# Attention and a SiLU feed-forward on one core: other byte offsets between the operands that TensorE streams and the weights that it loads

## The chip, the cores and the metric

The kernel runs on one core of a Trainium2 chip. The metric is device time in microseconds (us) of one execution, as the median of several. Lower is better.

## The reference

Eight batches of eight heads, 576 tokens, head size 64, go through attention with a mask by blocks of 64; the 4608 tokens of 512 features that come out go through a feed-forward with SiLU, without a bias. All is float32.

```python
B, H, S, D = q.shape                      # 8, 8, 576, 64
scores = (1.0 / np.sqrt(D)) * np.matmul(q, k.transpose(0, 1, 3, 2))
mask = (pos[:, None] // 64) >= (pos[None, :] // 64)
scores = np.where(mask, scores, -1000000000.0)
attn = np.exp(scores - np.max(scores, axis=-1, keepdims=True))
attn = attn / (np.sum(attn, axis=-1, keepdims=True) + 1e-09)
x = np.matmul(attn, v).transpose(0, 2, 1, 3).reshape(B * S, H * D)
h = x @ w_in                              # 4608x512 by 512x2048
out = (h / (1.0 + np.exp(-h))) @ w_out    # 4608x2048 by 2048x512
```

## The kernel before, in words

All instructions stand in one written order, the table `ORDER`; each word of it calls one method, and each engine works through its own instructions in that order. Float32 operands of the two feed-forward products are split into a high part in the rounded type float32r and a low part (the rest), and a product is made of three matmuls: high by high, high by low, low by high.

**Features and W_in.** `wi` (W_in, high and low, 64 KiB each in a partition) stays in SBUF throughout. Behind it stands a gap of `HALF_LINE` = 16 floats (64 bytes), and then `xbuf`, 64 KiB, that holds the features x. All pieces of W_in that TensorE loads start at a multiple of 256 bytes from the start of `wi`, and all pieces of x at a multiple of 256 bytes from the start of `xbuf`, so that x lies at 64 bytes from W_in modulo 256. The last 448 tokens of each batch are a group ("b", b): `x_batch(b)` gives its place, batch after batch in the two halves of `xbuf` in turn, as 4 chunks of features by high and low by 448 tokens (1792 bytes, 7 times 256). `x_hi` (ACT, L853) and `x_lo` (GpSimd, L856) write it once for two heads. The first 128 tokens of all batches make four more blocks of 256 tokens, which `x_batch` doesn't place.

**First product.** `ffn1` (the word `ffn` in `ORDER`, L1096) does a step: for a batch and one of 16 pieces of 128 columns of W_in, 12 matmuls of 128x128 weights from `wi` and 448 streamed columns from x, in two halves. A batch has 16 steps, 192 matmuls; eight batches have 1536 of the 1968 matmuls of L1096. `keep` takes a step's result out of PSUM, `save` sends it to DRAM.

**Attention.** For each of 64 heads, `scores` (L739) does ten matmuls: five pieces of the queries' columns (448, 320, 192, 448 and 64), each first with the high part `qh` and then with the low part `ql`, and with the keys, which lie in the same tile as `qh`, as the weights that are loaded. In that tile queries and keys are a multiple of 256 bytes apart; `ql` stands 64 bytes further (L723).

**Second product.** Here the parts of W_out stream and the features g are loaded. W_out is stored as eight double steps (`Turned`, d = 0 to 7) of two times seven blocks of 256 columns: d = 0 and 1 in tiles `ta`, d = 2 to 6 in tiles `tb`, d = 7 in the first half of `xbuf`. An `Item` is a quarter of a block of 256 tokens; it has two double steps, d = 2q and 2q + 1 for its quarter q, and puts its features into one of five places in turn: four in `wi`, which is no longer needed, and a fifth in the second half of `xbuf` (`slots`, L1190). `prod` (L1185) does one of the item's seven products: five of them are four matmuls in the order of 512, 512, 256 and 256 streamed columns, two are six of 256. There are 72 items; in the last four all products have six of 256.

```python
    def slots():
        if not spare:
            spare.extend([of_wi(d, d + 1) for d in (0, 4, 2, 6)] + [of_x(8, HALF_LINE)])
        return spare
```

Before, all of W_out lies at 64 bytes from `wi` modulo 256, and at 192 from the fifth place.

Of the kernel before, what the change touches and what calls it, by code (L numbers as in the profile page):

```python
# [10 lines left out]
F32R = mybir.dt.float32r  # L11
# [9 lines left out]
P = 128  # L21
NQ = S - 2 * D
# [9 lines left out]
CT = DM // P  # L32
# [41 lines left out]
PRODUCTS = [(1, 0), (2, 1), (6, 5), (5, 3), (7, 4), (3, 6), (4, 2)]  # L74
LAST = [(1, 0), (6, 5), (7, 4), (5, 3), (2, 1), (3, 6), (4, 2)]
HALF_LINE = 16
NARROW = (3, 4)
WIDE_WALKS = {"a": (0, 1, 2, 3), "b": (0, 2, 1, 3), "c": (1, 0, 3, 2)}
NARROW_WALKS = {"a": (0, 1, 2, 3, 4, 5), "b": (0, 3, 1, 4, 2, 5)}
WALKS = ("bb bb bb bb",)  # L80
FACTOR = {5: 0, 7: 1, 6: 2, 4: 3, 1: 4, 2: 5, 3: 6}

# [388 lines left out]
def attn_ffn(ctx: ExitStack, tc: tile.TileContext, qk, v, qk0, v0, qk1, v1, w_in, w_out, out):  # L471
# [14 lines left out]
    def bank(i):  # L486
        return pS.tile([P, 512], F32, tag=f"S{i}", name=f"S{i}")
# [5 lines left out]
    wi = [wboth[:, t] for t in range(2)]  # L493
    fp.tile([P, HALF_LINE // 2], F32, tag="gap", name="gap")
    cp.tile([P, HALF_LINE], F32, name="gap")
    xbuf = cp.tile([P, NX, 2, TB], F32R, name="x")
# [11 lines left out]

    def x_batch(b):
        half = xbuf[:, 8 * (b % 2) : 8 * (b % 2) + 8].rearrange("p n i t -> p (n i t)")  # L510
        return half[:, : CT * 2 * NQ].rearrange("p (c i t) -> p c i t", c=CT, i=2)

    def x_of(g, c, i):
        if g[0] == "b":
            return x_batch(g[1])[:, c, i]
        x = xbuf[:, 4 * g[0] + c, i, :]
        return x if len(g) == 1 else two(x, 4 * 2 * TB)
# [89 lines left out]
    def groups(seven):  # L607

        return [seven[:, 0:2], seven[:, 2:3], seven[:, 3:5], seven[:, 5:7]]
# [5 lines left out]
    def of_wi(d, e):  # L615

        a, b = slice(256 * d, 256 * d + 256), slice(256 * e, 256 * e + 256)
        return [[w[:, 0:2, a], w[:, 2:3, a], w[:, 0:2, b], w[:, 2:4, b]] for w in wi]

    def of_x(n, o):  # L620

        t = xflat[:, 2 * TB * n + o : 2 * TB * (n + 7) + o].rearrange("p (k i t) -> p k i t", i=2, t=TB)
        return [groups(t[:, :, i]) for i in range(2)]

    class Turned:
# [10 lines left out]
        def place(u):  # L636
            if u.d < NTA:
                t = pools["ta"].tile([P, 2, 7, 256], F32R, tag=f"ta{u.d}", name="ta")
                u.g = [groups(t[:, i]) for i in range(2)]
            elif u.d < 7:  # L640
                t = sp.tile([P, 2, 7, 256], F32R, tag=f"tb{u.d}", name="tb")
                u.g = [groups(t[:, i]) for i in range(2)]
            else:
                u.g = of_x(0, 0)
# [46 lines left out]
    class Unit:  # L691
# [30 lines left out]
        def split_q(u):  # L722
            u.ql = sp.tile([P, 512 + HALF_LINE], F32R, tag="ql", name="ql")[:, HALF_LINE : HALF_LINE + NQ]  # L723
            nc.gpsimd.tensor_tensor(out=u.ql, in0=u.raw[:, :NQ], in1=u.qh[:, :NQ], op=ALU.subtract)  # L724
            u.kk = u.qh[:, NQ:]
# [36 lines left out]
        def spread(u):  # L762
            for a in range(1, 4):
                copies[COPIES[1]](out=u.m[32 * a : 32 * a + 32], in_=u.m[:32])
# [85 lines left out]
        def x_hi(u):  # L850
            own(("b", u.b), u.h // 2)
            u.x = x_batch(u.b)[:, u.h // 2]
            nc.scalar.copy(u.x[:, 0], u.xu)  # L853
# [255 lines left out]
    class Item:  # L1109
# [53 lines left out]
        def prod(u, i):  # L1163
# [4 lines left out]
            o = z.o[pr]  # L1168
            second = z.wide and pr == NARROW[1]
            runs = []  # L1170
# [10 lines left out]
            kind = WALKS[u.blk % len(WALKS)].split()[u.q]  # L1181
            order = WIDE_WALKS[kind[0]] if len(runs) == 4 else NARROW_WALKS[kind[1]]
            for n, k in enumerate(order):
# [6 lines left out]
# [5 lines that stand above are left out]
    class Out:  # L1195
# [7 lines left out]
        def spread(u, pr):  # L1203
            return u.wide and pr not in NARROW

        def place(u, pr):

            if pr == NARROW[1]:
                return u.both[:, HD:] if u.wide else bank(3)
            if pr in (2, NARROW[0]):  # L1210
                t = pH.tile([P, 512], F32, tag="h", name="c2")
                if pr == NARROW[0]:
                    u.both = t
# [70 lines left out]
    a, b = First(0), First(1)  # L1284
# [24 lines left out]
    for token in ORDER.split():  # L1309
        name, _, method = token.partition(".")  # L1310
        if name.startswith("warm:"):
            warm(int(name[5:]))
        elif method:
            method, _, k = method.partition(":")
# [47 lines left out]
```

## Time and profile before

| what | value |
|---|---|
| median of 3 runs | 973.15 us (972.49 to 973.54) |
| profiled execution | 971.61 us, span in the trace 969.9 us |
| PE (matmuls) | 960.1 us busy, 99% of the span |
| PEld (weight loads) | 842.4 us, 87% |
| DVE, ACT, POOL | 810.0 us (84%), 688.4 us (71%), 644.1 us (66%) |
| granted clock of TensorE | 1.0 of full speed (2.4 GHz) |

The profiled execution is one of the kernel's executions; it lies 1.5 us under the median of the runs. A matmul's busy time in the trace runs from its start to its modelled end, and matmuls follow each other much more closely than that: for what a matmul costs, the distance between the starts of two of them counts. PE is TensorE's matmuls, PEld its weight loads, which overlap the matmuls; DVE is VectorE, ACT ScalarE, POOL GpSimd.

### The profile page before, as it was taken

Reading aid. Unit: us, or ns where it says so; the run is one execution under the profiler, and the core shown is the slowest. Engines: PE = TensorE matmul, PEld = TensorE weight load, DVE = VectorE, ACT = ScalarE, POOL = GpSimd, SP = SyncE. Lnnn points to the kernel's source line nnn. Section 1 sums busy time; section 2 is a strip of 40 time slices with the busy share of each in tenths; the row PEclk is TensorE's granted clock in tenths of the full one; section 3 lists DMA queues with packets and bytes.
Section 4 is the critical chain, followed back from the end, with each engine's and each line's share of the span. In section 5 each row is a group of like instructions: output and inputs, shape, how many; then the busy total and the mean of one; then the engine's idle time right before and its main releaser. Section 6 shows DMA issues by size and latency. Waiting matters only on the chain.

```text
span 969.9 us, 19538 instructions
## 1 busy us (share of the span) xinstructions
PE 960.1 (99%) x6258; PEld 842.4 (87%) x6258; DVE 810.0 (84%) x2001; ACT 688.4 (71%) x1525; POOL 644.1 (66%) x774
## 2 busy tenths in 40 slices
PE   7999999999999999999999999999999999999998
PEld 7778778888898888888888899999999999999998
DVE  6987898998999989999998766688888886888872
ACT  4867777777777777777777556887777776767760
POOL 5648887787778878778777634465654654565541
PEclk9999999999999999999999999999999999999999
DMA  9965555555555555555555356654555455445521
GB/s 352 384 179 180 152 154 145 156 165 147 150 156 152 155 157 153 159 152 150 159 159 153 112 190 207 198 173 131 129 160 152 136 149 147 131 120 153 142 66 44
DMA packets 109798, 155.42 MB, mean 160 GB/s; under 512 B 18560, under 2 KB 83072, under 8 KB 109696
## 3 DMA queue, kind: packets, MB, share of 16 engines
q1 hardware_dynamic: 109696, 154.18, 53.4%
q8 instruction: 49, 0.80, 0.3%
q14 instruction: 53, 0.43, 0.1%
HBM read 106.95 MB, written 47.19 MB: 159 GB/s over the span
## 4 chain that ended last, share of the span: by engine, by line
PE 95%; ACT 1%; DMA 1%; DVE 1%; POOL 1%; SPq 0%; issue 0%; POOLq 0%; DVEq 0%; ACTq 0%
PE h L1096 40%; PE c L1185 20%; PE S L1185 16%; PE S L739 9%; PE U L844 5%; PE SC L844 4%; DMA qk<-in_qk_dram 1%; PE S L1024 1%; PE S L1065 0%; PE S L901 0%; ACT MR L1038 0%; POOL wi L604 0%; POOL T L974 0%; POOL MR L894 0%; POOL wi L569 0%
## 5 line engine op out<-in xcount | busy, mean ns | idle before, releaser
L1096 PE MATMUL h<-x,wi 128*128 128x448 f32 (+2 forms) x1968 | 415.5, 367 | 0.0
L1096 PEld LDWEIGHTS h<-x,wi 128*128 128x128 f32 x1968 | 357.1, 188 | 32.2 <-issue 0.7
L1161 POOL TENSOR_TENSOR wi<-raw,wi 128x512 fp32r<-128x512 f32 (+1 forms) x116 | 117.8, 1030 | 110.7 <-ACT wi L1157 90.8
L678 DVE TRANSPOSE_TENSOR_REDUCE Mx<-S 64x4 f32<-64x128 f32 (+4 forms) x384 | 130.0, 396 | 6.0 <-PE S L739 4.9
L793 ACT ACTIVATE p<-T 128x512 f32<-128x512 f32 (+1 forms) x192 | 114.9, 613 | 27.4 <-DVE T L782 18.0
L1185 PE MATMUL c<-tb,wi 128*128 128x256 f32 (+1 forms) x727 | 129.2, 300 | 0.0
L799 POOL TENSOR_TENSOR pa<-p 128x448 f32<-128x448 f32 x64 | 73.8, 1153 | 60.5 <-ACT p L793 58.4
L1102 ACT COPY g<-h 128x448 f32<-128x448 f32 (+1 forms) x160 | 86.5, 541 | 37.5 <-PE h L1096 24.6
L1185 PEld LDWEIGHTS c<-tb,wi 128*128 128x128 f32 x727 | 107.0, 188 | 5.7
L1185 PE MATMUL S<-tb,wi 128*128 128x512 f32 (+1 forms) x456 | 100.4, 330 | 0.0
L720 POOL TENSOR_TENSOR qh<-qk,qh 64x576 fp32r<-64x576 f32 x64 | 91.3, 1427 | 8.4 <-POOL pa L802 3.0
L739 PE MATMUL S<-qh 128*128 128x448 f32 (+3 forms) x320 | 92.6, 304 | 0.0
L1124 ACT ACTIVATE raw<-raw 128x1024 f32<-128x1024 f32 x72 | 76.1, 1063 | 19.7 <-DMA raw<-gdb 16.5
L739 PE MATMUL S<-ql,qh 128*128 128x448 f32 (+3 forms) x320 | 83.7, 306 | 0.0
L1185 PEld LDWEIGHTS S<-tb,wi 128*128 128x128 f32 x456 | 75.9, 188 | 8.6
L714 ACT CAST qh<-qk 128x1024 fp32r<-128x1024 f32 x64 | 67.0, 1047 | 21.6 <-PE S L739 8.1
L724 POOL TENSOR_TENSOR ql<-qk,qh 128x448 fp32r<-128x448 f32 x64 | 73.8, 1154 | 3.4 <-ACT qh L714 0.4
L785 DVE TENSOR_TENSOR T<-S,MR 128x256 f32<-128x256 f32 (+2 forms) x192 | 73.5, 409 | 0.0
L739 PEld LDWEIGHTS S<-ql,qh 128*128 128x128 f32 (+1 forms) x320 | 56.9, 178 | 6.7 <-POOL ql L724 0.3
L739 PEld LDWEIGHTS S<-qh 128*128 128x128 f32 (+1 forms) x320 | 56.8, 177 | 3.3
L802 POOL TENSOR_TENSOR pa<-pa,p 128x320 f32<-128x320 f32 x64 | 55.9, 873 | 4.8
L1157 ACT CAST wi<-raw 128x512 fp32r<-128x512 f32 (+1 forms) x116 | 57.0, 516 | 1.8 <-PE c L1185 1.5
(187 smaller groups left out, 1859.8 us busy)
## 6 DMA issues: line engine op xcount, KB each, us to landing
qk<-in_qk_dram SPq DMA_DIRECT2D x128, 256.0 KB, 3.9
gdb<-g SPq DMA_DIRECT2D x128, 224.0 KB, 2.2
raw<-gdb SPq DMA_DIRECT2D x64, 256.0 KB, 3.4
v<-in_v_dram SPq DMA_DIRECT2D x64, 160.0 KB, 2.6
wst<-in_moe_w_in_dram SPq DMA_DIRECT2D x16, 512.0 KB, 8.8
wst<-in_moe_w_out_dram SPq DMA_DIRECT2D x16, 512.0 KB, 3.9
gd<-g SPq DMA_DIRECT2D x32, 256.0 KB, 3.5
raw<-gd SPq DMA_DIRECT2D x32, 256.0 KB, 3.6
```

The lines of the kernel that those rows point to most:

```text
L678: nc.vector.tensor_reduce(out=out, in_=in_, axis=AX.X, op=op, apply_transpose=True)
L720: nc.gpsimd.tensor_tensor(out=u.qh[r, c], in0=u.raw[r, c], in1=u.qh[r, c], op=ALU.subtract)
L724: nc.gpsimd.tensor_tensor(out=u.ql, in0=u.raw[:, :NQ], in1=u.qh[:, :NQ], op=ALU.subtract)
L739: nc.tensor.matmul(u.ps(c, w, m), u.kk[r, j * P : j * P + m], q[r, q0 : q0 + w], start=qq == 0 and not (ROWS and seg == 2), stop=qq == 1 a ...
L793: nc.scalar.activation(u.p[:, c:e], u.T[:, c:e], AF.Exp, scale=SCALE)
L799: nc.gpsimd.tensor_tensor(out=u.pa, in0=u.p[:, :NQ], in1=u.p[:, 960 : 960 + NQ], op=ALU.add)
L844: nc.tensor.matmul(U[64 * e : 64 * e + 64, q0 : q0 + w], y.vv[:, e, j], z.p[:, c : c + w], start=n == 0, stop=n == 4)
L1096: nc.tensor.matmul(o, w, x, start=half == 0 and i == 0 or f is None and i == 0, stop=(half == 1 or f is None) and i == len(runs) - 1)
L1102: nc.scalar.copy(g, hs.pop(z)[:, :n])
L1124: nc.scalar.activation(u.raw, u.raw, AF.Silu)
L1161: e.tensor_tensor(out=u.goal(1, k), in0=u.source(k), in1=u.goal(0, k), op=ALU.subtract)
L1185: nc.tensor.matmul(to, a, b, start=u.q == 0 and n == 0 and not second, stop=u.q == 3 and n == len(runs) - 1, skip_group_check=True)
```

## The change

The same instructions stand in the same order on each engine, and wait for the same things; what differs is the addresses of some operands. `x_batch` starts each batch a number of floats later (`XPLACE`), and the tiles `tb` are larger by a number of floats that stand unused ahead of the data (`WPLACE`), which also moves the tiles behind them. Two tables of walks lose entries that aren't used.

```diff
@@ -74,9 +74,11 @@
 HALF_LINE = 16
+XPLACE = (40, 4, 24, 2, 16, 1, 8, 0)
+WPLACE = {2: 32, 3: 0, 4: 48, 5: 0, 6: 48}
 NARROW = (3, 4)
-WIDE_WALKS = {"a": (0, 1, 2, 3), "b": (0, 2, 1, 3), "c": (1, 0, 3, 2)}
-NARROW_WALKS = {"a": (0, 1, 2, 3, 4, 5), "b": (0, 3, 1, 4, 2, 5)}
+WIDE_WALKS = {"a": (0, 1, 2, 3), "b": (0, 2, 1, 3)}
+NARROW_WALKS = {"b": (0, 3, 1, 4, 2, 5)}
@@ -508,7 +510,8 @@
     def x_batch(b):
         half = xbuf[:, 8 * (b % 2) : 8 * (b % 2) + 8].rearrange("p n i t -> p (n i t)")
-        return half[:, : CT * 2 * NQ].rearrange("p (c i t) -> p c i t", c=CT, i=2)
+        o = XPLACE[b]
+        return half[:, o : o + CT * 2 * NQ].rearrange("p (c i t) -> p c i t", c=CT, i=2)
@@ -638,7 +641,9 @@
             elif u.d < 7:
-                t = sp.tile([P, 2, 7, 256], F32R, tag=f"tb{u.d}", name="tb")
+                n = 2 * 7 * 256
+                t = sp.tile([P, n + WPLACE[u.d]], F32R, tag=f"tb{u.d}", name="tb")[:, WPLACE[u.d] :]
+                t = t.rearrange("p (i k n) -> p i k n", i=2, k=7)
```

In bytes, modulo 256, the operand that streams lies from the weights that are loaded at:

| first product, batch | 0 | 1 | 2 | 3 | 4 | 5 | 6 | 7 |
|---|---|---|---|---|---|---|---|---|
| before | 64 | 64 | 64 | 64 | 64 | 64 | 64 | 64 |
| now | 224 | 80 | 160 | 72 | 128 | 68 | 96 | 64 |

| second product, double step | 0, 1 | 2, 3 | 4, 5 | 6, 7 |
|---|---|---|---|---|
| from features in `wi`, before | 64 | 64 | 64 | 64 |
| from features in `wi`, now | 64 | 192 | 128 | 64 |
| from the fifth place, before | 192 | 192 | 192 | 192 |
| from the fifth place, now | 192 | 64 | 0 | 192 |

## Rows read from the trace of the kernel before

**Rows 1.** The page's head, its busy times, and PE, PEld and the granted clock in 40 equal slices of the span, in tenths.

```profile
span 969.9 us, 19538 instructions
PE 960.1 (99%) x6258; PEld 842.4 (87%) x6258; DVE 810.0 (84%) x2001; ACT 688.4 (71%) x1525; POOL 644.1 (66%) x774
PE   7999999999999999999999999999999999999998
PEclk9999999999999999999999999999999999999999
```

**Rows 2.** The chain of work that ended last, as shares of the span by engine.

```profile
PE 95%; ACT 1%; DMA 1%; DVE 1%; POOL 1%; SPq 0%; issue 0%; POOLq 0%; DVEq 0%; ACTq 0%
```

**Rows 3.** PE's waits in the whole span: who was waited for, us in total, times, longest us. The first and the last of seven rows.

```profile
PE S L945 <- DMA qk<-in_qk_dram: 3.4, 3, 1.5
...
PE U L986 <- ACT p L904: 0.2, 1, 0.2
```

**Rows 4.** The same chain in order of time, around the end of the attention: start in us, length in us, what, and how many instructions in a row. A length is from the start of the first to the start of what follows.

```profile
541.92 1.56 PE S L739 x10
543.49 7.29 PE h L1096 x36
...
555.89 62.61 PE h L1096 x312
618.50 0.69 PE S L1185 x4
```

**Rows 5.** Groups of PE's matmuls by line and shape: out<-in, size of the array used, streamed operand, count, busy us in all, mean ns of one, idle time before them. Of two names behind the arrow one streams and one is loaded; `S<-qh` streams from the tile that it loads from, `S<-ql,qh` streams `ql`.

```profile
L1096 PE MATMUL h<-x,wi 128*128 128x448 f32 x1536 | 320.3, 365 | 0.0
L739 PE MATMUL S<-qh 128*128 128x448 f32 x128 | 49.0, 383 | 0.0
L739 PE MATMUL S<-ql,qh 128*128 128x448 f32 x128 | 46.7, 365 | 0.0
L739 PE MATMUL S<-qh 128*128 128x320 f32 x64 | 19.7, 307 | 0.0
L739 PE MATMUL S<-ql,qh 128*128 128x320 f32 x64 | 19.7, 307 | 0.0
L739 PE MATMUL S<-ql,qh 128*128 128x192 f32 x64 | 17.4, 271 | 0.0
L739 PE MATMUL S<-qh 128*128 128x192 f32 x64 | 16.2, 254 | 0.0
L739 PE MATMUL S<-ql,qh 128*64 128x64 f32 x64 | 14.1, 221 | 0.0
L739 PE MATMUL S<-qh 128*64 128x64 f32 x64 | 12.3, 193 | 0.0
```

**Rows 6.** The same view, matmuls of the second product: `tb,wi` streams a tile `tb` against features in `wi` (64 bytes), `tb,x` against the fifth place (192 bytes).

```profile
L1185 PE MATMUL c<-tb,wi 128*128 128x256 f32 x587 | 92.7, 278 | 0.0
L1185 PE MATMUL S<-tb,wi 128*128 128x512 f32 x210 | 68.5, 391 | 0.0
L1185 PE MATMUL c<-tb,wi 128*128 128x512 f32 x140 | 45.7, 391 | 0.0
L1185 PE MATMUL c<-tb,x 128*128 128x256 f32 x138 | 21.0, 277 | 0.0
L1185 PE MATMUL S<-tb,x 128*128 128x512 f32 x45 | 14.7, 392 | 0.0
L1185 PE MATMUL c<-tb,x 128*128 128x512 f32 x30 | 9.8, 392 | 0.0
```

**Rows 7.** PE's matmuls of one head's scores in order of time: start us, us, what.

```profile
469.48 0.37 PE L739 MATMUL S<-qh 128*128 128x448 f32 x1
469.69 0.36 PE L739 MATMUL S<-ql,qh 128*128 128x448 f32 x1
469.89 0.30 PE L739 MATMUL S<-qh 128*128 128x320 f32 x1
...
470.38 0.39 PE L739 MATMUL S<-qh 128*128 128x448 f32 x1
470.61 0.36 PE L739 MATMUL S<-ql,qh 128*128 128x448 f32 x1
```

**Rows 8.** The weight loads of the same stretch.

```profile
469.49 0.19 PEld L739 LDWEIGHTS S<-ql,qh 128*128 128x128 f32 x1
...
470.29 0.19 PEld L739 LDWEIGHTS S<-qh 128*128 128x128 f32 x1
470.40 0.19 PEld L739 LDWEIGHTS S<-ql,qh 128*128 128x128 f32 x1
```

**Rows 9.** Instructions that write or read the tile `x`: the two that write a batch's features, with minimum, median and maximum ns, first and last start in us.

```profile
L853 ACT CAST x<-xu x32: 558/567/571, 122.4 to 557.5; 128x448 fp32r<-128x448 f32 x32
L856 POOL TENSOR_TENSOR x<-xu,x x32: 1140/1156/1172, 123.6 to 558.1; 128x448 fp32r<-128x448 f32 x32
```

**Rows 10.** Busy time of each engine in one stretch of 60 us of the attention, about one batch long.

```profile
240.00:300.00 60.00, 60.00 (x349) 51.58 (x348) 55.26 (x165) 46.05 (x118) 48.17 (x62) 1.00 0.55 151
```

## The prediction

> **What bounds the kernel now.** I read the page's head first. PE is busy 99% of the span, from the second of 40 slices on in nearly every slice, and the granted clock is 1.0, which is 2.4 GHz [rows 1]. The chain that ended last is PE for 95% [rows 2]. PE's waits come next: of seven the longest is 3.4 us, on the first loads, and the rest are all on lines of the early attention [rows 3]; no later matmul waits for another engine. So the kernel is one long row of matmuls, and its time is the sum of the distances from one start to the next. Whatever a matmul's distance gains or loses comes out at the end one for one.
>
> The mean ns of a group of matmuls is not that distance. The chain has 312 matmuls of the first product, 448 streamed columns each, in 62.61 us [rows 4], or 200.7 ns each, where their mean is 365 ns [rows 5]: 164 ns more. For the second product the chain has four matmuls (two of 512 columns, two of 256) in 0.69 us [rows 4]; their means add up to 2 x 391 + 2 x 278 = 1338 ns [rows 6], which is 4 x 162 ns more than 690. So a mean is the distance plus about 163 ns, whatever the number of columns, and **the difference between two means is the difference between two distances**. That lets the means by shape be compared.
>
> At 2.4 GHz 448 columns at one a clock take 186.7 ns. The distance of 200.7 ns is 14 ns more. The four matmuls of the second product have 1536 columns, 640 ns, and take 690, 12.5 ns more each. This surplus is what an operand's place could give back, at most.
>
> **What the change moves.** No instruction is added, removed or moved in its order, and no wait. What differs is where TensorE's streamed operand starts against the weights that are loaded, in 1344 matmuls of the first product (seven batches of 192; batch 7 stays at 64) and, in the second, for double steps 2 to 5. For those an item has 5 x 4 + 2 x 6 = 32 matmuls, and the last block's 42, so that a pair of double steps has 17 x 32 + 42 = 586.
>
> **What the rows say of an offset.** Three offsets occur before: 0, 64 and 192.
>
> *0 against 64.* The scores stream `qh` at 0 to the keys that are loaded, and `ql` at 64. With 320 columns both take 307 ns [rows 5]. With 448 columns it is 383 against 365 ns, with 192 it is 254 against 271, with 64 it is 193 against 221. These don't mean that 0 is dearer: the five of a head add up to 2 x 383 + 307 + 254 + 193 = 1520 ns at 0, and to 2 x 365 + 307 + 271 + 221 = 1529 ns at 64, 9 ns less at 0 over 1472 columns. The 18 ns at 448 columns come from the second of the two. The first one's distance to the next start is 469.69 - 469.48 = 0.21 us, the second one's 470.61 - 470.38 = 0.23 us [rows 7]. It stands behind the two of 192 columns, whose weight loads can't be had faster than about 0.11 us apart, so that the load behind it starts 0.02 us after it (470.40) instead of with it (469.49 against 469.48) [rows 7, 8]. That shift is the whole difference.
>
> *192 against 64.* Streaming against the fifth place takes 277 ns with 256 columns where `wi` takes 278, and 392 with 512 where `wi` takes 391 [rows 6].
>
> So three offsets 64 bytes or more apart agree within about 2 ns of 200. By them the offset doesn't matter.
>
> **The sum.** For double steps 2 and 3, which go to 192: ten of 512 columns at +1 ns and 22 of 256 at -1 ns give -12 ns per item, times 17, and 42 at -1 ns in the last block: -0.25 us; a fifth of the items go the other way, from 192 to 64, which leaves about -0.2 us. Double steps 4 and 5 at 128 (and 0 from the fifth place) have no row; the nearest on either side, 64 and 192, bound them at 0 and -0.2 us, and I take -0.1 us. The largest difference that any row shows, +18 ns, and the whole surplus, -12.5 ns, give +10.5 and -7.3 us for these 586. For the first product no row shows 224, 80, 160, 72, 128, 68 or 96. I take 0 for all, since 0, 64 and 192 are the nearest and agree; the bounds are the surplus, 1344 x -14 ns = -18.8 us, and 1344 x +18 ns = +24.2 us. 128 is bracketed by 64 and 192 and the safest of them; 68 to 96, 160 and 224 are not multiples of 64, which no streamed operand of float32r in the rows is.
>
> The other engines write the moved tiles. Of a batch's features ACT writes four times 567 ns and GpSimd four times 1156 ns [rows 9]. Were each twice as long at its new start, that is 2.3 and 4.6 us per batch, in a stretch of 60 us in which ACT has 14 and GpSimd 12 us to spare [rows 10], and no matmul waits there for them [rows 3]: nothing at the end. That cover would be gone if PE were waiting for features, and then at most 7 x 4 x 1.16 = 32 us would show; nothing in the rows points to it. The loads and casts of W_out's tiles are ahead of their use in the same way; their addresses stay multiples of 64 bytes, and I cost them at nothing.
>
> The sum is -0.3 us: on the profiled execution, 971.6 us, 971.3. That execution lies 1.5 us under the median of the runs, 973.15, and on the median the sum is **972.9 us**. I take 0.2%, 2 us, as what a measurement of this kernel can tell from no change.
>
> The Trainium skill's page "TensorE: Matmul & The Clock Gate" says under "Step-by-step: what each phase is for" that TensorE reads the streamed operand and the loaded weights through two independent ports, and that loading the next weights takes no read bandwidth from the running matmul. By that alone no offset could matter and the change would be worth 0. Under "Back-to-back issue gap" it gives N/2.4 + 2.5 ns, 189.2 ns for 448 columns as an estimate from that page; the trace has 200.7 ns, so something else does take 11.5 ns, and the measurement decides. The faster rival lives on that.
>
> **Rivals.**
>
> *Slower: streams that start off a multiple of 64 bytes stumble.* The place is batches 0, 1, 2, 3, 5 and 6, 1152 matmuls, whose features start 32, 16, 32, 8, 4 and 32 bytes behind one. For it: all rows of the streamed operand are at multiples of 64, so their agreement says nothing of these; and a surplus of 14 ns shows that reading isn't free. Against: three quite different offsets differ by no more than about 2 ns. From 2 us / 1152 = 1.7 ns each, under 1% of a distance, it decides. With a quarter of the bound, 4.5 ns, it costs 5.2 us: 978 us. The Trainium skill's page "SBUF — State Buffer", section "Door 1: The DMA port swizzle", states lines of 16 bytes, with a penalty for each access that crosses into a new one. By that the starts at 72 and 68 would need 113 lines where 112 did, an estimate of 1.8 ns each in 384 matmuls, or 0.7 us, under what can be told; no row shows such a start.
>
> *Faster: the surplus is a collision that 64 doesn't avoid best.* Streaming and loading go on at once, and some of the new offsets could make them meet less. For it: the 14 ns, and the 1 ns at 256 columns. Against: 0 and 192 give nothing back at 448 or 512 columns. From 1.5 ns in 1344 matmuls it decides; a third of the surplus, 4.7 ns, gives 6.3 us: 967 us.
>
> *The change does something, but its parts cancel.* Each batch has its own offset, so some may gain and some lose: 5 ns in one batch is 192 x 5 ns = 1 us. This ends within 2 us unless most have one sign, and I count it to no change.
>
> **How the numbers follow.** No change (972.9 us, by itself 971 to 975) 0.48; slower 0.30, since six of eight batches go where no row is; faster 0.22. The range of 8 in 10 reaches from 968.5 us (3.3 ns per matmul gained; 0.08 lies below) to 979.5 us (5.7 ns in 1152 lost; 0.11 above).
>
> **What would show it.** Right: in the profile after, the means by shape of L1096 with 448 columns and of L1185 stay within 1 or 2 ns of 365, 278 and 391, each batch's 192 matmuls keep 200 to 201 ns apart, and PE has no new waits. The slower rival shows as a mean above 366 ns for L1096 alone, and batch by batch as longer distances where the start is off a multiple of 64; the faster one as distances nearer to 187 ns. It would be wrong in another way if a wait for features or W_out appeared behind L853, L856 or L1185, or if a distance depended on the batch in the order of its offset, which would show that the offset counts after all.

## The result, and the profile after

The changed kernel takes 979.46 us (median of three runs, 979.43 to 980.24) where the kernel before takes 973.15: 1.0068 times as long, 95% interval 1.0045 to 1.0091. It is slower by 6.3 us. The forecast was no change, 972.9 us; the result lies at the upper end of the range, and the rival that ended slower had 978 us.

The page of the changed kernel, its head, its busy times, PE and the granted clock in 40 slices, and the first shares of the chain by engine:

```profile
span 977.7 us, 19538 instructions
PE 967.9 (99%) x6258; PEld 844.8 (86%) x6258; DVE 811.3 (83%) x2001; ACT 689.0 (70%) x1525; POOL 643.8 (66%) x774
PE   7999999999999999999999999999999999999998
PEclk9999999999999999999999999999999999999999
PE 94%; DMA 3%; DVE 1%; POOL 0%; ACT 0%; issue 0%; SPq 0%; POOLq 0%; ACTq 0%; DVEq 0%
```

Beside [rows 1, 2] nothing new appears: as many instructions, PE busy 99%, the chain PE. But PE is busy 7.8 us longer, which is just what the span gained (977.7 - 969.9). The other engines' busy times hardly move (DVE +1.3, ACT +0.6, POOL -0.3 us), so the writes of the moved tiles cost nothing.

The profile says 0.998 for the mean granted clock, against 1.000 before. The dip is in the first 20 us (0.91 there, 1.00 in the stretches behind), where the loads set the time: counted from the span's start, the first matmul of the eight batches' 1536 starts at 157.4 us in the changed kernel and at 157.8 us before. Of the 7.8 us, 5.0 have gathered where the second product begins (623.3 against 618.3 us), and 2.8 come in the second product.

PE's waits in the changed kernel, the first row and the only new one of eight (us in total, times, longest us):

```profile
PE S L950 <- DMA qk<-in_qk_dram: 3.3, 3, 1.3
PE c L1190 <- ACT g L1107: 0.3, 1, 0.3
```

The first is that of [rows 3]. The new one lies in the first item of the second product, where two products in a row take 1110 and 819 ns in place of 693 and 707: half a microsecond, far too small to be the loss. So the matmuls themselves must stand further apart. The groups by shape in the changed kernel (columns as in [rows 5, 6]; its lines are five further down):

```profile
L1101 PE MATMUL h<-x,wi 128*128 128x448 f32 x1536 | 325.6, 369 | 0.0
L1190 PE MATMUL c<-tb,wi 128*128 128x256 f32 x587 | 92.8, 279 | 0.0
L1190 PE MATMUL S<-tb,wi 128*128 128x512 f32 x210 | 68.9, 393 | 0.0
L1190 PE MATMUL c<-tb,wi 128*128 128x512 f32 x140 | 46.0, 394 | 0.0
L1190 PE MATMUL c<-tb,x 128*128 128x256 f32 x138 | 21.5, 279 | 0.0
```

The 1536 matmuls of the first product went from 365 to 369 ns, the second product's from 278 to 279, from 391 to 393 and 394, and from 277 to 279 [rows 5, 6]. Batch by batch it is plainest in the chain, in order of time (start us, length us, what), here in one stretch of batch 5, whose features stand at 68. First the kernel before, then the changed one:

```profile
490.96 1.41 PE S L739 x10
...
500.30 6.09 PE h L1096 x30
506.38 1.41 PE S L739 x10
507.79 4.89 PE h L1096 x24
```

```profile
494.17 1.41 PE S L744 x10
...
503.55 6.34 PE h L1101 x30
509.89 1.41 PE S L744 x10
511.30 5.08 PE h L1101 x24
```

The heads' scores between, whose operands have not moved, keep their 1.41 us for ten matmuls. Thirty matmuls of the first product take 6.34 us instead of 6.09, 24 take 5.08 instead of 4.89: 8 ns more each. The same pieces for batches 0 to 4, one of each, in the changed kernel:

```profile
186.00 6.22 PE h L1101 x30
...
238.85 6.18 PE h L1101 x30
...
297.79 6.11 PE h L1101 x30
...
370.56 6.21 PE h L1101 x30
...
444.08 6.20 PE h L1101 x30
```

Every batch that has moved is longer than 6.09, batch 2 (offset 160) by least. A piece holds a hand-over to the next line too. Free of it is the mean distance from one start to the next, worked out from the starts of the single matmuls in the trace, without those that another line follows and without those of 280 ns and more; 173 to 191 of a batch's 192 are left. Before, it is 200.0 to 200.2 ns in all eight batches. After:

| batch | 0 | 1 | 2 | 3 | 4 | 5 | 6 | 7 |
|---|---|---|---|---|---|---|---|---|
| offset | 224 | 80 | 160 | 72 | 128 | 68 | 96 | 64 |
| distance, ns | 204.2 | 203.5 | 200.7 | 204.4 | 203.8 | 208.7 | 205.3 | 200.1 |

Each less 200.1, times 192 and added up, is +5.7 us. That is a little too much: of the 1536 distances the 1436 counted here grew by 5.3 us in all, and the 100 at hand-overs did not grow. Batch 7 stayed at 64 and at 200.1.

### The profile page after: what moved, and what is told of

Read it like the earlier page. It is cut to its first block, busy times and chain, and to the rows that moved or that the text cites. A ratio compares the mean times of both kernels' runs of the same rounds, so it can differ in the third digit from the quotient of the medians.

```text
span 977.7 us, 19538 instructions
## 1 busy us (share of the span) xinstructions
PE 967.9 (99%) x6258; PEld 844.8 (86%) x6258; DVE 811.3 (83%) x2001; ACT 689.0 (70%) x1525; POOL 643.8 (66%) x774
## 4 chain that ended last, share of the span: by engine, by line
PE 94%; DMA 3%; DVE 1%; POOL 0%; ACT 0%; issue 0%; SPq 0%; POOLq 0%; ACTq 0%; DVEq 0%
PE h L1101 40%; PE c L1190 20%; PE S L1190 15%; PE S L744 9%; PE U L849 5%; PE SC L849 4%; DMA wst<-in_moe_w_in_dram 2%; DMA gd<-g 1%; DMA qk<-in_qk_dram 1%; PE S L1029 0%; DMA gdb<-g 0%; PE S L1070 0%; PE S L906 0%; DVE wm L595 0%; POOL x L676 0%
## 5 line engine op out<-in xcount | busy, mean ns | idle before, releaser
L1101 PE MATMUL h<-x,wi 128*128 128x448 f32 (+2 forms) x1968 | 420.8, 370 | 0.0
L1101 PEld LDWEIGHTS h<-x,wi 128*128 128x128 f32 x1968 | 357.8, 188 | 36.4 <-issue 0.7
```

The source lines that it names most:

```text
L1101: nc.tensor.matmul(o, w, x, start=half == 0 and i == 0 or f is None and i == 0, stop=(half == 1 or f is None) and i == len(runs) - 1)
```

## The experiments

Diffs are against the changed kernel. "Distance" is always the mean of one batch as above. Times of the kernel before are from runs beside the experiment, on the same chip. Of e3, e4, e5, e7, e9, e10 and e11 there is one execution each, so their times stand without an interval and the argument goes by the distances in their traces.

### Which of the two parts costs what

`e1_features_only` moves the features and leaves W_out in its place:

```diff
-WPLACE = {2: 32, 3: 0, 4: 48, 5: 0, 6: 48}
+WPLACE = {2: 0, 3: 0, 4: 0, 5: 0, 6: 0}
```

> Only the features' starts are changed as in the changed kernel; W_out's tiles stand as before. Theory A (the place of the streamed features against W_in sets a matmul's distance, batch by batch): the distances of the changed kernel come back, 204.2, 203.5, 200.7, 204.4, 203.8, 208.7, 205.3 and 200.1 ns for batches 0 to 7 against 200.1 before, which over 192 matmuls each is 5.7 us more than before, and that is nearly all of the loss. Theory B (W_out's tiles or the waits behind them make most of the loss): under 2 us more than before.

`e2_wout_only` moves W_out and leaves the features:

```diff
-XPLACE = (40, 4, 24, 2, 16, 1, 8, 0)
+XPLACE = (0, 0, 0, 0, 0, 0, 0, 0)
```

> Only W_out's tiles are moved as in the changed kernel; the features start as before. Theory A: all batches at 200.1 ns; the second product's quarter 2 (double steps 4 and 5, at 128) is dearer by 1.6 us in all, the other quarters together by well under 1 us, so 1.5 to 2.5 us more than before. Theory B: 4 us or more.

Features only: 977.69 us against 972.48, ratio 1.0053 (1.0041 to 1.0066), +5.2 us. W_out only: 974.5 us, 1.0022 (1.0013 to 1.0031), +2.0 us. Each batch's distance under features only is that of the table above within 0.1 ns. With W_out only, all batches are back at 200.0 to 200.2, and the second product takes 350.4 us from the start of its first product to the start of its last, as in the changed kernel (350.2), where the kernel before has 347.4. So both parts lose, each by itself, and the first product's offsets make nearly three quarters of it; the sum, 7.2 us, lies within the interval of the whole change (4.4 to 8.9 us).

### The batch or its offset

`e3_other_batches` gives the same eight offsets to other batches, W_out back in its place (as in e4 to e7, e9 and e10):

```diff
-XPLACE = (40, 4, 24, 2, 16, 1, 8, 0)
+XPLACE = (4, 40, 2, 24, 1, 16, 0, 8)
```

> The same eight starts of the features, given to other batches: 80, 224, 72, 160, 68, 128, 64 and 96 bytes for batches 0 to 7. W_out as before. If the offset sets the distance: 203.5, 204.2, 204.4, 200.7, 208.7, 203.8, 200.1 and 205.3 ns. If it is the batch (its place in the program, what the other engines do at the time, or its half of the features' tile): batch 5 stays near 208.7 and batch 4 near 203.8 whatever the offset.

The chain's pieces of batches 0 to 5 with these places (80, 224, 72, 160, 68, 128):

```profile
186.68 6.18 PE h L1101 x30
...
246.98 6.22 PE h L1101 x30
...
312.62 6.21 PE h L1101 x30
...
371.59 6.11 PE h L1101 x30
...
445.18 6.33 PE h L1101 x30
...
504.72 6.19 PE h L1101 x30
```

The 6.11 has gone with offset 160 to batch 3, the 6.33 with 68 to batch 4. The distances by offset are those of the table within 0.3 ns, and the run took 977.49 us (features only: 977.69). The offset sets the distance, not the batch.

`e4_other_offsets` sets 48, 32, 0, 240, 192, 208, 112 and 144 (and W_out back), `e7_fine_offsets` 60, 56, 176, 168, 152, 164, 76 and 156:

```diff
-XPLACE = (40, 4, 24, 2, 16, 1, 8, 0)
+XPLACE = (60, 56, 48, 44, 32, 36, 12, 20)
```

> Eight offsets that no batch had: 48, 32, 0, 240, 192, 208, 112 and 144 bytes for batches 0 to 7. W_out as before. If only starts off a multiple of 64 bytes are dear: 0 and 192 stay at 200 ns, and the other six lie at 203 to 209. If each offset modulo 256 has a distance of its own by how streaming and loading meet: no such split, with 0 or 192 as likely dear as the others, since 128, a multiple of 64, is at 203.8 and 160, which is none, at 200.7.

```diff
-XPLACE = (40, 4, 24, 2, 16, 1, 8, 0)
+XPLACE = (63, 62, 28, 26, 22, 25, 3, 23)
```

> Eight more offsets: 60, 56, 176, 168, 152, 164, 76 and 156 bytes for batches 0 to 7, W_out as before. If the distance is smooth in the offset with low places at 64 and 160: the five around 160 between 200.5 and 203 ns, 60 and 56 between 200 and 203. If 64 and 160 are single low places with dear neighbours, as 68 is to 64: 60, 156 and 164 at 205 ns or more.

They took 976.97 us (against 972.48) and 977.22 us (against 972.06). The two decisive offsets are 0 and 192, the ones that the forecast leaned on. In e4 they are batches 2 and 4, here 0 at 311.75 and 192 at 443.85, with 240 between:

```profile
311.75 6.16 PE h L1101 x30
...
370.66 6.16 PE h L1101 x30
...
443.85 6.15 PE h L1101 x30
```

All three are longer than the 6.09 that the first product has at 64; their distances are 202.6, 202.7 and 202.3 ns. In this product's own stream, 0 and 192 do not agree with 64. Ordered by where the streamed operand starts within 16 bytes, all that the first product has shown so far (W_in at a multiple of 64):

| start within 16 bytes | offset: distance in ns |
|---|---|
| 0 | 64: 200.1; 160: 200.7; 192: 202.3; 0: 202.6; 240: 202.7; 48: 202.9; 32: 203.1; 80: 203.5; 128: 203.8; 208: 204.0; 224: 204.2; 176: 204.3; 96: 205.3; 112: 206.5; 144: 206.6 |
| 4 | 68: 208.7; 164: 207.1 |
| 8 | 72: 204.4; 56: 203.3; 152: 204.8; 168: 206.3 |
| 12 | 60: 200.9; 76: 201.2; 156: 202.2 |

Among the multiples of 16 there is a spread of 6.5 ns. Off them, 4 bytes on is dear, and 12 bytes on nearly as cheap as the best. Neither picture of e7 came out: 60 and 156 stayed cheap, 164 and 168 did not.

### Does it add up

`e6_all_68` gives all batches the dearest offset so far:

```diff
-XPLACE = (40, 4, 24, 2, 16, 1, 8, 0)
+XPLACE = (1, 1, 1, 1, 1, 1, 1, 1)
```

> All eight batches at 68 bytes, W_out as before. If the distance belongs to the offset and all of it comes out at the end: 1536 matmuls at 208.7 instead of 200.1 ns, 13.1 us more than before, about 985.6 us on a median of 972.5. If part of it is taken up by waits that shrink elsewhere: clearly less than 11 us.

The group of the first product, and two of its pieces:

```profile
L1101 PE MATMUL h<-x,wi 128*128 128x448 f32 x1536 | 332.8, 373 | 0.0
```

```profile
186.37 6.34 PE h L1101 x30
...
508.25 6.33 PE h L1101 x30
```

The mean is 8 ns above [rows 5], the distance 208.8 to 208.9 ns in all batches, which makes 1536 x 8.8 = 13.5 us. Measured: 984.02 us against 972.06, ratio 1.0121 (1.0104 to 1.0138), +12.0 us. The price is per matmul and the same in every batch, and it goes to the end nearly whole. What is missing of 13.5 is mostly that not all 1536 pay: the 1436 distances without a hand-over grew by 12.5 us, the 100 at hand-overs by nothing. In the trace the second product begins 12.0 us later than before.

### Offset to the loaded weights, or start in memory

`e5_win_moved` moves W_in by 4 bytes, so that the same offsets have other starts; the features' buffer stays where it is:

```diff
-XPLACE = (40, 4, 24, 2, 16, 1, 8, 0)
+XPLACE = (25, 17, 9, 5, 2, 3, 1, 0)
...
-    wboth = cp.tile([P, 2, CT, DFF], F32R, name="wi")
+    wboth = cp.tile([P, 2 * CT * DFF + HALF_LINE], F32R, name="wi")[:, 1 : 1 + 2 * CT * DFF].rearrange("p (t c f) -> p t c f", t=2, c=CT)
...
-    cp.tile([P, HALF_LINE], F32, name="gap")
```

> W_in itself starts 4 bytes later in its tile, and the features' starts are chosen so that they lie at 160, 128, 96, 80, 68, 72, 64 and 60 bytes from it for batches 0 to 7. Against a line of 64 bytes they start at 36, 4, 36, 20, 8, 12, 4 and 0 bytes. If the offset between the two operands sets the distance: 200.7, 203.8, 205.3, 203.5, 208.7, 204.4 and 200.1 ns for batches 0 to 6, as where W_in stood 4 bytes earlier; 60 is not known. If the streamed operand's own start sets it (64-byte lines): batches 1 and 6, which start 4 bytes behind one, at 208.7, batch 4, 8 bytes behind, at 204.4, and batch 7, on one, at 200.1. W_out stands as before, so 60 instead of 64 from the features in W_in's place: up to 2 us in the second product, not told apart here.

`e9_win_32` moves it by 32 bytes, so that all starts stay multiples of 16 but shift against 64:

```diff
+XPLACE = (32, 28, 24, 20, 16, 12, 8, 0)
...
+    wboth = cp.tile([P, 2 * CT * DFF + HALF_LINE], F32R, name="wi")[:, 8 : 8 + 2 * CT * DFF].rearrange("p (t c f) -> p t c f", t=2, c=CT)
```

> W_in starts 32 bytes later in its tile; the features lie at 160, 144, 128, 112, 96, 80, 64 and 32 bytes from it for batches 0 to 7. All starts are multiples of 16 bytes. If, among such starts, the offset between the two operands sets the distance, the numbers found at those offsets come back: 200.7, 206.6, 203.8, 206.5, 205.3, 203.5, 200.1 and 203.1 ns. If the features' own place in SBUF sets it, the numbers found at those places come back: 202.3, 204.3, 200.7, 206.6, 203.8, 206.5, 205.3 and 200.1 ns. The batches 6 and 7 tell it best. The second product has W_out at 32 instead of 64 bytes in this kernel, which e8 found dearer by about 1 us for a quarter of it.

`e11_start_4` leaves W_in and puts all features 4 bytes past a multiple of 16, and parts of W_out 4, 8 and 12 bytes past one:

```diff
+XPLACE = (61, 57, 49, 41, 33, 17, 13, 5)
+WPLACE = {2: 1, 3: 1, 4: 2, 5: 2, 6: 3, 7: 3}
...
-                u.g = of_x(0, 0)
+                u.g = of_x(0, WPLACE[u.d])
```

> The features of all batches start 4 bytes behind a multiple of 16, at 52, 36, 4, 228, 196, 132, 116 and 84 bytes from W_in. If a start 4 bytes into 16 is dear wherever it lies, as at 68 and 164: all eight between 205 and 209 ns. If 68 and 164 are dear for their own offsets: spread as the others, with some at 203 or less. In the second product W_out's double steps 2 and 3 start 4 bytes, 4 and 5 start 8 bytes, and 6 and 7 start 12 bytes behind a multiple of 16; by the first theory 2 and 3 are dearest, a product of six 256s at 715 ns or more against 693 before, and 6 and 7 nearly as before.

e5, 984.99 us against 972.06: offset 68, with its start now 8 into 16, fell from 208.7 to 202.5 ns; 64, with its start 4 into 16, rose from 200.1 to 206.9, and 160 from 200.7 to 205.5. So the offset alone does not set the distance. The start alone does not either: 128, 96 and 80 at a start of 4 all came out at 207.8 to 208.0, but 60, whose start is a multiple of 64, at 203.4, where that theory had 200.1. The time holds more than the first product: from the features in W_in's place W_out lies at 60 in this kernel, and the second product takes 4.7 us longer, where up to 2 were expected.

e9, 980.34 us against 972.62, keeps all starts at multiples of 16. Its pieces for offsets 160, 144 and 128 (batches 0 to 2):

```profile
186.71 6.10 PE h L1100 x30
...
246.93 6.28 PE h L1100 x30
...
312.75 6.20 PE h L1100 x30
```

Seven of the eight distances are again those of the table within 0.5 ns: 160 at 200.7, 144 at 206.6, 128 at 203.7, 112 at 206.7, 96 at 205.2, 80 at 203.1, 64 at 200.1. Their starts against 64 bytes have changed by 32, so among multiples of 16 it is the offset to the weights that counts, and a grid of 64 bytes doesn't explain it. The eighth, 32, misses: 206.6 here, 203.1 in e4. It is also the only one of the eight that is not the same whole distance: 32 bytes here, 288 in e4, alike only modulo 256. So the period may be longer than 256 bytes; no run tests that, and it stays open. Of the 7.7 us that e9 is slower, 2.3 are in the second product.

e11, 991.8 us against 972.62, all starts at 4 into 16: 206.4 to 207.8 ns in seven batches (36, 52, 116, 132, 196, 228 and 4), whatever the offset, and 219.9 ns at 84. Two rows show the last one, batches 5 and 7 in the chain:

```profile
506.99 6.28 PE h L1101 x30
...
599.80 31.02 PE h L1101 x141
```

6.28 us for 30 is 209 ns with the hand-over; 31.02 us for 141 is 220 ns. With a start of 4 into 16 the distance is 6 to 8 ns above 200.1 at nearly every offset, and the offset's own price doesn't show. Why 84 costs 20 was not found. The second product does it in part: W_out 4 into 16 takes 714.4 ns per product of four and 722.4 per six, and 12 into 16 takes 695.6 and 699.1. But 8 into 16 is as dear there as 4, 715.9 and 722.8, against the expectation and unlike the first product.

### Which load it is

Of the three matmuls of a product the first two use W_in's high part; while the second runs, the low part is loaded for the third. `e10_low_32` moves the low part alone by 32 bytes:

```diff
-    wi = [wboth[:, t] for t in range(2)]
+    wi = [wboth[:, t * CT * DFF + o : t * CT * DFF + o + CT * DFF].rearrange("p (c f) -> p c f", c=CT) for t, o in enumerate((0, 8))]
...
+XPLACE = (20, 20, 12, 12, 8, 8, 0, 0)
```

> Only the low parts of W_in start 32 bytes later, the high parts as before, so that the features lie at 144, 144, 112, 112, 96, 96, 64 and 64 bytes from the high parts and at 112, 112, 80, 80, 64, 64, 32 and 32 from the low ones. Of three matmuls the first and second use the high part and the third the low one; the low part is loaded while the second runs. If the load that runs during a matmul counts: in batches 4 and 5 the second of three is cheap (about 200 to 202 ns) and the first and third near 205; in 6 and 7 the second is the dear one (203). If its own weights count: the third is the odd one out. If neither counts and only the features' own place does: all three as where the high part alone gives the offset, 205 to 206 in batches 4 and 5, and 198 to 202 in batches 6 and 7.

It took 982.43 us against 972.62. The distance by place in the three, worked out from the same starts:

| offset to the high / low part | first | second | third | the same with one offset for both |
|---|---|---|---|---|
| 96 / 64 (batches 4, 5) | 204.4 | 201.2 | 207.6 | 96: 204.9, 205.5, 205.2; 64: 198.3, 201.8, 200.1 |
| 64 / 32 (batches 6, 7) | 203.6 | 206.5 | 202.9 | 32: 207.0, 205.9, 206.9 (e9) |
| 112 / 80 (batches 2, 3) | 203.6 | 204.4 | 204.9 | 112: 206.7, 206.8, 206.8; 80: 203.2, 203.1, 202.9 |
| 144 / 112 (batches 0, 1) | 205.7 | 198.9 | 199.5 | 144: 206.8, 206.5, 206.6 |

In the first two rows the second matmul does what the low part's offset does (201.2 as at 64, where it is 197.5 to 202.0 from batch to batch; 206.5 as at 32 in e9), as it would if the load that runs while it streams counted. But its neighbours shift too (203.6 where 64 has 198.3), and 144 / 112 gives 198.9 and 199.5 although 144 and 112, each for both parts, have 206.5 to 206.8. So a distance is not a table of one matmul's offset: the neighbours' addresses enter, and the experiment supports the load that runs meanwhile without settling how the two meet. The loads' own records hardly grow: their median is 188 ns before and in the changed kernel, and 190 in e6, where the distance has grown by 8.8. Of e10's 9.8 us, 5.2 are in the second product, which puts its features where W_in's parts were.

### The second product

`e8_wout_other` puts its double steps at 160 (2, 3), 32 (4, 5) and 240 (6, 7), the features of the first product at 64:

```diff
+XPLACE = (0, 0, 0, 0, 0, 0, 0, 0)
+WPLACE = {2: 24, 3: 0, 4: 32, 5: 0, 6: 52, 7: 44}
...
-                u.g = of_x(0, 0)
+                u.g = of_x(0, WPLACE[u.d])
```

> The features start as before; W_out's double steps 2 and 3 lie at 160, 4 and 5 at 32, 6 and 7 at 240 bytes from the features in W_in's place (and 32, 160 and 112 from the fifth). If the second product goes by the same table as the first: 160 as cheap as 64 (a product of six near 690 ns, of four near 690), 32 and 240 dearer by 2 to 3 ns a matmul, about 3 us more than before in all. If the table is another for 256 and 512 columns: 160 need not be cheap; a total within 1 us of before, or under it, would be a version to go on with.

976.2 us against 972.06, ratio 1.0043 (1.0028 to 1.0058), +4.1 us; the second product takes 351.7 us, 4.3 more than before. The best new offset of the first product, 160, is the dearest in this table. In ns per product of four matmuls (two of 512, two of 256 columns) and of six of 256, over a quarter's 70 and 28 products with features in W_in's place:

| offset | four | six |
|---|---|---|
| 64 (before) | 690.0 | 693.3 (either 680 or 706) |
| 192 (changed kernel) | 695.5 | 680.0 |
| 128 (changed kernel) | 699.8 | 709.0 |
| 160 (e8) | 702.8 | 712.5 |
| 32 (e8) | 695.3 | 699.9 |
| 240 (e8) | 697.3 | 702.9 |

At 64, products of six take turns between 680 and 706 ns; at 192 they are at 680 throughout. In the kernel before, the dear items are, but for the last block, those with features in the first and third place, so the turns could be a matter of place. The first item, in e6 and before, says otherwise: W_out and the features lie the same in both, only the first product ahead of it differs. Its last sixteen matmuls (one product of four and two of six), before and in e6:

```profile
621.26 2.11 PE c L1185 x16
```

```profile
633.26 2.05 PE c L1190 x16
```

Its products of six take 707 and 706 ns before and 680 in e6, and the three items behind it are exchanged in the same way. So the addresses alone don't set the value: something of what ran ahead carries over, and what that is was not found.

As 192 showed only the cheap value, `e12_wout_192` puts all of W_out at 192, from the fifth place too:

```diff
+XPLACE = (0, 0, 0, 0, 0, 0, 0, 0)
+WPLACE = {0: 0, 1: 32, 2: 32, 3: 0, 4: 0, 5: 0, 6: 0, 7: 32}
...
-                t = pools["ta"].tile([P, 2, 7, 256], F32R, tag=f"ta{u.d}", name="ta")
+                n = 2 * 7 * 256
+                t = pools["ta"].tile([P, n + WPLACE[u.d]], F32R, tag=f"ta{u.d}", name="ta")[:, :n]
...
-            spare.extend([of_wi(d, d + 1) for d in (0, 4, 2, 6)] + [of_x(8, HALF_LINE)])
+            spare.extend([of_wi(d, d + 1) for d in (0, 4, 2, 6)] + [of_x(8, HALF_LINE + 32)])
```

> Features as before; all of W_out at 192 bytes from the features of the second product, the fifth place included. By the products already seen at 192 (693.4 ns for four, 680 for six, against 690.0 and 693.3 at 64) an item takes 9.6 ns less in four of five items: 0.5 to 0.8 us less than before in all, under what a measurement can tell. If the table found for single products doesn't add up: a time more than 1 us off.

Two neighbouring items in the chain, sixteen matmuls in a row of each (one product of four and two of six), before and in e12:

```profile
703.46 2.11 PE c L1185 x16
...
708.32 2.05 PE c L1185 x16
```

```profile
703.92 2.05 PE c L1192 x16
...
708.74 2.05 PE c L1192 x16
```

The dearer of the two values, 2.11, is gone, and products of six stay at 680 ns in all four quarters. Products of four pay for it: 693.3 instead of 690.0. The second product takes 346.6 us, 0.8 less than before. The time is 971.43 us against 972.62, ratio 0.9992 (0.9983 to 1.0001): the fastest of all kernels here, and not told from no change.

## Why the prediction was wrong, and where it was right

**The step that failed** is the price of the first product: "For the first product no row shows 224, 80, 160, 72, 128, 68 or 96. I take 0 for all, since 0, 64 and 192 are the nearest and agree". The measured term is +5.3 us in place of 0 (+5.2 on the median of e1). The agreement was real, but it was seen in other streams: 0 against 64 in the scores, 192 against 64 in the second product [rows 5, 6]. Neither carries over. In the first product's own stream 0 costs 2.5 ns and 192 costs 2.2 ns more than 64 (e4), and the second product orders the offsets in another way altogether (160 is next to the best in the one and the dearest in the table of the other). Offsets that agree in one stream were no bracket for another. And the agreement in the second product was one of means: the 278 ns at 64 in [rows 6] mix products of six at 680 and at 706 ns, while at 192 all are at 680, in the same trace. The unit of the argument could have warned: 1344 matmuls times 1.5 ns is the 2 us that can be told, so rows known to within 2 ns could not bear a forecast of no change.

**128**, called "bracketed by 64 and 192 and the safest of them", cost 3.7 ns in the first product and, in the second, most of the loss: 10 ns per product of four, 16 ns per product of six, together +1.6 us in its quarter.

**The second product** was forecast at -0.3 us and measured at +2.0 (e2; its distances give +3.0, the upper end of the interval). The -1 ns at 256 columns had the right side for 192: products of six fell from 693 to 680 ns, 2 ns for each matmul. But products of four rose from 690.0 to 695.5, more than the +1 ns of each of their 512-column matmuls, so this quarter lost too (87.0 us before, 87.3 in the changed kernel). The quarters that have not moved lost 0.5 and 0.4 us. In the first the loss is the new wait in the first item, without which its products of four keep their 690 ns. In the last, at the same 64, they took 695.4 instead of 690.0. That this comes from the items ahead, whose W_out has moved, is argued from e6, where a product's value depends on what ran ahead of it; no run isolates it here.

**The slower rival** had the right side and, by luck, nearly the right sum (5.2 us over 1152 matmuls; measured 5.3 over 1344): its 4.5 ns for each batch was near the mean of prices from 0.6 to 8.6, and its 978 us had no loss in the second product. It had not the right mark. It put the loss on starts off a multiple of 64. 128, a multiple, costs 3.7 ns; 160, which is none, 0.6; and e9 shifted all starts by 32 against 64 bytes without changing seven of eight distances. Nor did it stay with L1096 alone, as the forecast had it for this rival: the means of the second product rose too. What does count of the start is its place within 16 bytes (e5, e11). The Trainium skill's page "SBUF — State Buffer", section "Door 1: The DMA port swizzle", speaks of lines of 16 bytes and a penalty for crossing into another. The measurement agrees in that the place within 16 bytes counts, but counting lines doesn't give the price: starts of 4, 8 and 12 into a line all need one line more, and have distances of 205.5 to 219.9, 202.5 to 206.3 and 200.9 to 202.2 ns.

**The faster rival** found nothing in the first product: of all offsets tried there, none is below 64.

**Parts that cancel** did not: none of the seven moved batches gained.

**What was right.** That the kernel is a row of matmuls, and that a distance goes to the end one for one: 7.8 us more of PE, 7.8 us more span. That a mean is a distance plus a constant, so that means compare: the mean of L1101 rose by 4 ns, as the distances did on average (200.1 to 203.8 ns). That the writes of ACT and GpSimd cost nothing. And the last of the signs named, a distance that depends on the batch in the order of its offset, is what appeared.

The forecast set the Trainium skill's rule of two independent read ports ("TensorE: Matmul & The Clock Gate", "Step-by-step: what each phase is for") beside its sum, and by that rule the change is worth 0. The measurement differs: with the first product's instructions and waits unchanged, 200.1 to 208.9 ns by the place of the streamed operand, and at multiples of 16 bytes by its place against the weights (e9). In this row of float32r matmuls streaming was not independent of where the loaded weights lie.

The reading of [rows 7, 8], by which the 18 ns between `qh` and `ql` at 448 columns is a shift left by the loads ahead and not the offset, was not tested; the scores' addresses were left alone in every run.

## What to carry to other kernels

In a kernel whose time is a row of matmuls, the byte distance between the streamed operand and the weights that are loaded during the stream is a size to be tuned, for each product by itself: it was worth up to 9 ns of 200 per matmul. Rows from another product with other widths and another order of loads don't price it; one run with a different offset in each batch prices eight of them at once. Keep starts at multiples of 16 bytes, which none of the dearest here were, and don't move a place that measured well to tidy it up.

## What the runs showed of the hardware that was not expected

- The distance of 448-column float32r matmuls depends on the offset between the streamed operand and the weights, without any wait in the trace: 200.1 ns (64) to 206.6 ns (144) at multiples of 16 bytes.
- A streamed operand that starts 4 bytes past a multiple of 16 takes 205.5 to 208.9 ns at all offsets but one, and 219.9 ns at 84; 12 bytes past takes 200.9 to 202.2. Neither the exception nor the difference between 4 and 12 is explained.
- The same product at the same addresses has two values, and which one it takes depends on what ran ahead: the first item's six of 256 columns at 64 take 707 ns before and 680 in e6. From item to item the two take turns. With all of W_out at 192 only the lower was seen.
- Moving W_in's low part alone by 32 bytes gave 198.9 and 199.5 ns to the second and third matmul of 144 / 112, where 144 and 112 for both parts give 206.5 to 206.8. A layout that uses this was not tried.
